# Other landing times in a kernel's build-time planner, and another table of planning parameters (attention block and gated feed-forward, one core)

## The chip, the core and the metric

The kernel runs on one core of a Trainium2 chip. The metric is the device time of one execution in microseconds. The core has TensorE (PE: matmuls, with its weight loads shown apart), VectorE (DVE), ScalarE (ACT), GpSimd (POOL) and SyncE (SP), each with a queue of its own that it works through in order. Nearly all transfers (DMAs) are issued by SP.

## The reference

For x of 2048 tokens by 512 features, in bf16:

```python
mod = (silu(c) @ w_mod)                # six rows of 512: sa, ca, ga, sb, cb, gb
h = layernorm(x) * (1 + ca) + sa
# 32 heads of 16: q, k, v = h @ wqkv; p = softmax(q k^T / 4); o = p v
x = x + ga * (o @ wo)
h = layernorm(x) * (1 + cb) + sb
x = x + gb * ((gelu(h @ w_gate) * (h @ w_up)) @ w_down)    # 512 -> 1792 -> 512
```

With 32 heads of only 16 features, the scores are 32 x 2048 x 2048 numbers that all have to be exponentiated. That is the main work.

## The kernel before

**Tiles.** The scores are cut into slots: 128 keys on the partitions by 512 columns (queries of one head, or two key tiles by 256 queries). There are 2048 slots. A round is four slots, one for each of four heads that share TensorE's array. The queries are cut into nine sets (`SETS`: seven of 256, two of 128); a unit is one set (or two merged) with one of eight head groups `qd` of four heads. For each unit the kernel goes through its rounds: scores into the PSUM tile `ps_sc`, exponential into `E`, and the product with the values into `ps_pv`; a seventeenth column of ones in the values (`vaug`) gives the softmax's sums.

**Two ways to exponentiate.** ACT takes two or three slots in one ACTIVATE (`E<-ps_sc`, 128x1024 or 128x1536; the helper's line is 377). Some rounds go to DVE instead, as one "quad": four TENSOR_SCALAR that read `ps_sc` and write uint16 bit patterns of an approximate power of two (128x512, line 389), and three more over 128x2048 that shift the bits (`shift_task`, line 1804). The four versions are weighted by scaled copies of the values (`vs`) in the product and so average out much of the approximation's error.

**Side work.** All else runs beside the scores, mostly through the PSUM tile `ps_mi`: layer norms and the projections to q, k and v of later groups, then, as sets of queries are done, the output projection, second layer norm and feed-forward of each set. The feed-forward of the first six sets streams its weights from HBM in double buffers. Exponentials of the GELU (a tanh) go to ACT as well (`wreg<-wreg`).

**The end of a unit** (`unit_end`, line 1826) normalises: the product with its sums is copied to `osb`; SP moves the sums to `den` ("db", spread over 128 partitions); DVE takes reciprocals into `rden`; SP stores them in HBM ("dc", `scr_rec<-rden`), and loads them back broadcast over 16 partitions in four pieces ("dd", `rb<-scr_rec`); DVE multiplies `osb` by `rb` into `onorm`. When the odd head groups of a set are there, SP moves them beside the even ones ("de", `onorm<-onorm`). The other names: "st" loads gate and up weights, "sd" loads scaled down weights; "se" loads the raw down weights, DVE scales them by gb, and "ws" stores them (`wd_scaled<-mreg`, seven times in a row, each after the one before, lines 995 to 1003).

**The planner.** No order is written out. When the program is built, `stream` (line 1441) places instructions one at a time on a modelled clock: it asks when each candidate could start (`probe`, line 327), takes one, and moves the clock of its engine on (`model`, line 297). The order that results is fixed in each engine's queue; at run time only semaphores hold it. For a DMA the clock has a time of issue (`ISSUE`) and a landing:

```python
self.free[eng] = t + ISSUE.get(op.stream[2:4], 450)                                   # 301
self.dma_free = max(t + 900, self.dma_free) + size / (320 if run >= 1024 else 245 if run >= 512 else 200)
op.t1 = self.dma_free + (1000 if run > 64 else 1500) + margin                          # 303
late = EARLY if qd < 6 else (0, 0, 0)                                                  # 1845, in unit_end
```

Here `margin` is the name's entry in `MARGIN` (nanoseconds; 0 if it has none), plus one of `EARLY`'s three numbers for the sums, the broadcasts and the merges of head groups below 6. A step that needs a transfer is placed on its engine's queue when the clock says that the transfer has landed (`step`, line 1312). A transfer that really lands later makes the engine stand at that step, with all that is queued behind it.

**The table.** `TUNE` has a row for each 64 slots (`rules(pos // 64)`, line 1634; rows are counted from 0, the last of the 33 stands for all beyond it). The 14 entries of a row, counted from 0:
- 0: how much work (ns) ACT must have ahead before side work or filling goes before scores
- 1: from slot 1536 on, the owed side work ("credit", in columns, at most 4096) below which a round may go to DVE
- 2: how many DVE steps may be waiting when a round is given to DVE
- 3: how long DVE may stand for a score bank before another step is put ahead
- 4 and 5: how far DVE's clock may be ahead of now (4) or of ACT's (5) when it takes scores
- 6 and 7: when the shifts of a round become urgent
- 8 and 9: how far ahead a round for DVE is picked, and how near to its unit's end it no longer is
- 10 and 11: how much credit side work needs to run, and to go ahead of scores
- 12: how fast credit accrues, in per cent
- 13: how far ahead DVE is given steps in the background

The line that gives a round to DVE (1668, cut) reads:

```python
if (len(mem) == CH or there) and c > 2 and self.free["dve"] < max(t + self.tune[4], self.free["act"] + self.tune[5]):
```

TensorE's activity is watched too: `short` (line 1427) sums the columns placed in the last 3413 ns of the clock, and where they are below `FILL` = 3700, idle stretches are filled with matmuls whose result isn't used (lines 1660 and 1755 to 1768).

Of the kernel before, what the change touches and what calls it, by code (L numbers as in the profile page):

```python
# [50 lines left out]
FLOW = sum(a + n <= 1536 for a, n in SETS)  # L51
ISSUE = {"dd": 462, "de": 630, "db": 610, "dc": 400, "st": 410, "sd": 530, "se": 530, "ws": 450, "wu": 420, "wg": 510, "wd": 480, "ou": 400, "qo": 620}
SAFE = 0
EARLY = (1500, 2500, 2000)
MARGIN = {"db": 1200, "dd": 1800, "de": 1500, "qo": 1500, "st": 1500, "sd": 1700, "se": 1700, "wd": 1700, "wu": 1500, "wg": 1500}
FIRST = (2, 1, 2, 3)
STOP = ('ln2',)
STOPAT = 0
# [2 lines left out]
STEP = 64  # L61
RULES = (600, 3500, 6, 120, 700, 150, 2, 9, 96, 30, 2, 1536, 100, 150)
TUNE = (
# [33 lines left out]
)  # L97
END = (0, None)
WAIT = 250
# [29 lines left out]
class _Recorder:  # L129
# [292 lines left out]
    def dma(self, eng, out, in_, sem, noncontig=False, late=0):  # L422
# [8 lines left out]
        run = min(int(a.ap[-1][1]) * mybir.dt.size(a.dtype) for a in (out, in_))  # L431
        return self.rec(eng, fn, [in_], [out], dma=sem, cost=(n, run, MARGIN.get(sem[:2], 0) + late))

# [36 lines left out]
class _Kernel(_Recorder):  # L470
# [967 lines left out]
    def rules(self, i):  # L1438
        self.tune = TUNE[min(i, len(TUNE) - 1)]

# [385 lines left out]
    def unit_end(self, u, acc):  # L1826
# [17 lines left out]
        sem = b + 4 * (o > 0)  # L1844
        late = EARLY if qd < 6 else (0, 0, 0)
        s2 = self.scr2[b, P * o:P * o + 4 * L]
# [261 lines left out]
```

## Time and profile before

| | us |
|---|---|
| runs shown (3) | 808.4, 812.86, 815.13 |
| median | 812.86 |
| the profiled execution | 810.3 |
| its span, first to last instruction | 808.6 |
| ACT busy | 776.8 |
| DVE busy | 752.3 |
| PE busy | 750.5 |
| mean granted TensorE clock | 0.996 |

Times in the profile are microseconds from the span's start. A group is written line, engine, operation, output<-inputs (buffer numbers left out), how many times. "Idle before" is the time in which the engine stood just ahead of such an instruction, with what released it. The helpers that record instructions each have one line (364 matmul, 377 activation, 389 tensor_scalar, 427 DMA), so groups are told apart by their tiles. Consecutive instructions of one engine overlap a little: their mean durations add up to more than the busy time.

### The profile page before, as it was taken

How to read it: one execution, taken by the hardware profiler on the slowest of the kernel's cores; microseconds unless marked ns; L12 is line 12 of the kernel's file. 1: busy time of each engine (PE TensorE's matmuls, PEld its weight loads, DVE VectorE, ACT ScalarE, POOL GpSimd, SP SyncE). 2: the span in 40 equal slices, each digit the busy share in tenths (PEclk: the TensorE clock that was granted, in tenths of full speed). 3: DMA queues.
4: the chain of work that ended last, by engine and by line, in shares of the span. 5: the costliest groups of instructions: out<-in, count | busy, mean ns of one | idle time of the engine just before them, and what ended most of it. 6: DMA issues, size and time to landing. Idle time of an engine off the chain costs nothing.

```text
span 808.6 us, 37540 instructions
## 1 busy us (share of the span) xinstructions
PE 750.5 (93%) x17260; PEld 374.8 (46%) x17264; DVE 752.3 (93%) x1521; ACT 776.8 (96%) x734; POOL 4.6 (1%) x13
## 2 busy tenths in 40 slices
PE   8899999998989998999999999988999999989998
PEld 4333334433544454444543554344434554446666
DVE  7877899999999999999999999999998999999973
ACT  6999999999999999999999999999999999999972
POOL 2000000000000000000000000000000000000000
PEclk9999999999999999999999999999999999999999
DMA  9100112221541144104420442043223622200000
GB/s 295 66 15 8 25 50 74 75 58 32 148 145 29 39 128 134 34 16 133 129 65 16 140 121 54 22 128 114 62 64 104 189 83 76 71 10 13 18 12 15
DMA packets 97904, 60.92 MB, mean 75 GB/s; under 512 B 16913, under 2 KB 95378, under 8 KB 97746
## 3 DMA queue, kind: packets, MB, share of 16 engines
q1 hardware_dynamic: 97216, 57.99, 25.2%
q8 instruction: 135, 2.21, 1.1%
q10 hardware_dynamic: 530, 0.53, 0.2%
q14 instruction: 23, 0.19, 0.1%
HBM read 51.74 MB, written 4.18 MB: 69 GB/s over the span
## 4 chain that ended last, share of the span: by engine, by line
ACT 81%; PE 13%; DVE 3%; DMA 2%; issue 1%; SPq 0%; DVEq 0%
ACT E L377 78%; PE ps_sc L364 5%; PE ps_mi L364 4%; PE ps_pv L364 3%; ACT wreg L377 3%; DMA scr_rec<-rden 1%; DMA xs<-in_A_x_dram 0%; DVE mreg L389 0%; DMA mreg<-in_B_w_up_dram 0%; SPq L427 0%; DMA rb<-scr_rec 0%; DVE st L417 0%; DVE wreg L398 0%; DVE hreg L389 0%; PE ps_mi L368 0%
## 5 line engine op out<-in xcount | busy, mean ns | idle before, releaser
L377 ACT ACTIVATE E<-ps_sc 128x1024 bf16<-128x1024 f32 (+2 forms) x688 | 750.8, 1295 | 17.8 <-PE ps_sc L364 17.2
L364 PE MATMUL ps_sc<-qo,kT 32*128 32x256 bf16 (+2 forms) x2048 | 202.0, 273 | 19.8 <-ACT E L377 17.6
L364 PE MATMUL ps_sc<-qT,kT 32*128 32x256 bf16 (+3 forms) x2048 | 202.0, 274 | 17.7 <-ACT E L377 14.3
L364 PE MATMUL ps_pv<-E,vaug 128*17 128x256 bf16 (+2 forms) x3168 | 151.5, 274 | 2.7 <-DVE vaug L398 1.1
L389 DVE TENSOR_SCALAR dreg<-ps_sc 128x512 uint16<-128x512 f32 x204 | 138.2, 687 | 4.6 <-PE ps_sc L364 4.0
L364 PE MATMUL ps_mi<-wreg,mreg 128*32 128x256 bf16 x2816 | 110.0, 275 | 5.2 <-DVE wreg L398 1.7
L364 PEld LDWEIGHTS ps_sc<-qT,kT 32*128 32x128 bf16 (+1 forms) x2048 | 62.7, 92 | 109.8 <-ACT E L377 89.4
L364 PEld LDWEIGHTS ps_sc<-qo,kT 32*128 32x128 bf16 x2048 | 63.1, 92 | 106.5 <-ACT E L377 87.7
L364 PEld LDWEIGHTS ps_pv<-E,vaug 128*17 128x17 bf16 x3168 | 61.0, 89 | 58.9 <-issue 40.8
L389 DVE TENSOR_SCALAR kq<-ps_sc 128x512 uint16<-128x512 f32 x112 | 76.3, 688 | 8.0 <-PE ps_sc L364 7.4
L364 PEld LDWEIGHTS ps_mi<-wreg,mreg 128*32 128x32 bf16 x2816 | 64.1, 96 | 38.6 <-issue 21.5
L364 PE MATMUL ps_pv<-mreg,vs 128*17 128x256 bf16 (+2 forms) x1544 | 69.6, 267 | 0.5 <-issue 0.5
L389 DVE TENSOR_SCALAR mreg<-ps_sc 128x512 uint16<-128x512 f32 x100 | 67.7, 687 | 1.7 <-PE ps_sc L364 1.2
L389 DVE TENSOR_SCALAR mreg<-dreg 128x2048 uint16<-128x2048 uint16 x91 | 61.5, 686 | 0.0
L364 PEld LDWEIGHTS ps_pv<-mreg,vs 128*17 128x17 bf16 x1544 | 35.2, 91 | 9.6 <-issue 3.4
L364 PE MATMUL ps_mi<-hreg,wreg 128*32 128x512 bf16 (+1 forms) x496 | 37.3, 382 | 0.4 <-DVE vaug L398 0.2
L381 DVE TENSOR_TENSOR wreg<-wreg 128x1024 bf16<-128x1024 bf16 (+1 forms) x56 | 34.6, 618 | 0.0
L394 DVE SCALAR_TENSOR_TENSOR wreg<-wreg,ps_mi 128x512 bf16<-128x512 bf16 x49 | 33.5, 683 | 0.6 <-PE ps_mi L364 0.2
L398 DVE CAST wreg<-ps_mi 128x512 bf16<-128x512 f32 x49 | 33.6, 686 | 0.5 <-PE ps_mi L364 0.2
L389 DVE TENSOR_SCALAR mreg<-mreg 128x2048 uint16<-128x2048 uint16 x46 | 31.1, 684 | 0.0
L389 DVE TENSOR_SCALAR mreg<-kq 128x2048 uint16<-128x2048 uint16 x45 | 30.7, 686 | 0.1
L377 ACT ACTIVATE wreg<-wreg 128x1024 bf16<-128x1024 bf16 (+1 forms) x28 | 29.8, 1065 | 0.0
(202 smaller groups left out, 786.9 us busy)
## 6 DMA issues: line engine op xcount, KB each, us to landing
mreg<-in_B_w_up_dram SPq DMA_DIRECT2D x46, 256.0 KB, 3.1
mreg<-in_B_w_gate_dram SPq DMA_DIRECT2D x42, 256.0 KB, 3.7
dreg<-wd_scaled SPq DMA_DIRECT2D x18, 256.0 KB, 3.4
rb<-scr_rec SPq DMA_DIRECT2D x116, 32.0 KB, 2.0
mreg<-wd_scaled SPq DMA_DIRECT2D x12, 256.0 KB, 4.2
ereg<-wd_scaled SPq DMA_DIRECT2D x12, 256.0 KB, 4.1
mreg<-in_w_mod_dram SPq DMA_DIRECT2D x1, 2048.0 KB, 12.2
out_dram<-xs SPq DMA_DIRECT2D x15, 128.0 KB, 2.0
```

What stands on the lines that cost most here:

```text
L364: return self.rec("pe", lambda e: e.matmul(out, lhsT, rhs, start=start, stop=stop, tile_position=tp), [lhsT, rhs], [out], cost=(n, int(rhs ...
L377: return self.rec("act", lambda e: e.activation(out, in_, func, scale=scale, **kw), rd, wr, cost=self.cost("act", out, [in_], "act"))
L381: return self.rec(eng, lambda e: e.tensor_tensor(out, a, b, op), [a, b], [out], cost=self.cost(eng, out, [a, b], "tt"))
L389: return self.rec(eng, lambda e: e.tensor_scalar(out, a, s1, s2, **kw), rd, [out], cost=self.cost(eng, out, [a], "ts") + 60 * (len(rd) - 1 ...
L394: return self.rec("dve", lambda e: e.scalar_tensor_tensor(out, a, s, b, op0=op0, op1=op1), rd, [out], cost=self.cost("dve", out, [a, b], " ...
L398: return self.rec(eng, lambda e: e.tensor_copy(out, in_), [in_], [out], cost=self.cost(eng, out, [in_], "ts"))
```

## The change

Only three constants change; no function does. `EARLY` and `MARGIN` hold the landing times that the planner's clock assumes, and `TUNE` is another table, found by a search that charged stretches with few TensorE columns. Since the planner places every instruction by them, the order in all queues after the first microseconds may differ, and so may the number of rounds that go to DVE. What is computed is the same, but for which rounds are exponentiated on which engine.

```diff
-EARLY = (1500, 2500, 2000)
-MARGIN = {"db": 1200, "dd": 1800, "de": 1500, "qo": 1500, "st": 1500, "sd": 1700, "se": 1700, "wd": 1700, "wu": 1500, "wg": 1500}
+EARLY = (800, 1000, 800)
+MARGIN = {"db": 1200, "dd": 1800, "de": 1500, "qo": 1500, "st": 2300, "dc": 1500, "ws": 1500, "sd": 2000, "se": 1700, "wd": 1700, "wu": 1500, "wg": 1500}
```

All rows of the table but a few change. These are rows 0 to 6, 15 to 19 and 29 to 32, the old ones first:

```diff
 TUNE = (
-    (600, 3500, 6, 120, 700, 150, 2, 9, 96, 30, 2, 1536, 100, 150),
-    (600, 3500, 6, 120, 700, 150, 2, 9, 96, 30, 2, 1536, 100, 150),
-    (600, 3000, 4, 120, 700, 300, 2, 9, 96, 30, 2, 1536, 80, 150),
-    (600, 3000, 5, 60, 700, 150, 2, 9, 96, 30, 2, 1536, 80, 150),
-    (600, 3000, 5, 60, 700, 150, 3, 9, 96, 30, 2, 1536, 125, 150),
-    (600, 3000, 5, 60, 1100, 150, 3, 9, 96, 30, 2, 1536, 80, 150),
-    (600, 3500, 6, 120, 900, 450, 2, 16, 64, 30, 2, 1536, 110, 150),
...
-    (600, 4097, 6, 200, 900, 150, 2, 9, 128, 38, 2, 1536, 125, 400),
-    (600, 4097, 6, 200, 900, 300, 2, 6, 128, 38, 2, 1536, 125, 150),
-    (600, 4097, 6, 0, 900, 300, 2, 6, 128, 34, 0, 1536, 125, 0),
-    (450, 4097, 6, 0, 900, 300, 2, 6, 48, 34, 0, 1536, 125, 0),
-    (450, 4097, 6, 0, 900, 300, 2, 6, 48, 34, 0, 1536, 125, 0),
...
-    (600, 3500, 6, 120, 700, 150, 2, 9, 96, 30, 2, 1536, 100, 150),
-    (1000, 3500, 6, 120, 500, 150, 2, 6, 96, 24, 2, 1536, 100, 150),
-    (450, 4097, 6, 300, 1100, -100, 1, 9, 96, 30, 4, 1536, 100, 150),
-    (450, 4097, 6, 300, 1100, -100, 1, 9, 96, 30, 4, 1536, 100, 150),
+    (1000, 4097, 6, 120, 700, 150, 2, 9, 96, 30, 2, 1536, 100, 150),
+    (600, 3500, 6, 120, 700, 150, 2, 3, 96, 38, 2, 1536, 100, 150),
+    (600, 3500, 6, 120, 1100, -100, 2, 6, 96, 27, 2, 1536, 100, 400),
+    (1000, 3500, 6, 120, 1100, 450, 3, 9, 96, 27, 2, 1536, 125, 400),
+    (1000, 3500, 6, 120, 1100, 450, 3, 9, 96, 27, 2, 1536, 125, 400),
+    (1000, 3500, 8, 120, 1100, 300, 3, 9, 96, 27, 2, 2500, 125, 400),
+    (1000, 3500, 8, 120, 1100, 300, 3, 9, 96, 27, 2, 2500, 125, 400),
...
+    (600, 3500, 6, 120, 700, 150, 0, 9, 96, 30, 2, 800, 100, 150),
+    (450, 3500, 6, 120, 700, 150, 0, 9, 96, 30, 2, 800, 100, 150),
+    (450, 2500, 6, 0, 700, 150, 0, 9, 128, 30, 1, 800, 125, 250),
+    (450, 2500, 7, 60, 700, 150, 0, 9, 128, 30, 1, 800, 125, 150),
+    (300, 2500, 10, 60, 700, 0, 0, 9, 128, 24, 1, 2500, 125, 150),
...
+    (600, 2500, 6, 0, 700, 450, 1, 9, 64, 27, 1, 1536, 125, 150),
+    (600, 2500, 3, 200, 1100, 450, 1, 3, 64, 27, 2, 1536, 125, 150),
+    (600, 3500, 6, 120, 700, 450, 2, 9, 96, 27, 0, 1536, 100, 150),
+    (600, 3500, 6, 120, 700, 450, 2, 9, 96, 27, 0, 1536, 100, 150),
 )
```

31 rows, old and new, of the table TUNE are left out of this document.

## The prediction, made before the changed kernel ran

> **What bounds the kernel now.** I read the page's head, then the busy time by stretch, then the waits by engine, then the chain of work. First the page:
>
> ```profile
> span 808.6 us, 37540 instructions
> PE 750.5 (93%) x17260; PEld 374.8 (46%) x17264; DVE 752.3 (93%) x1521; ACT 776.8 (96%) x734; POOL 4.6 (1%) x13
> ACT 81%; PE 13%; DVE 3%; DMA 2%; issue 1%; SPq 0%; DVEq 0%
> ```
>
> ScalarE (ACT) is busy for 96% and carries 81% of the chain. The stretches show where its other 4% lies. Columns: stretch, length, then busy time of PE, weight loads, DVE, ACT and POOL, the granted clock, DMA share and GB/s.
>
> ```profile
> 15.40:100.00 84.60, 77.58 (x1376) 29.43 (x1376) 70.06 (x184) 84.17 (x78) 0.31 (x1) 0.98 0.14 46
> 100.00:200.00 100.00, 93.65 (x2149) 40.44 (x2145) 97.41 (x190) 100.00 (x93) 0.00 (x0) 1.00 0.22 61
> 200.00:300.00 100.00, 93.15 (x2242) 47.89 (x2246) 96.72 (x183) 98.80 (x94) 0.00 (x0) 1.00 0.34 97
> 300.00:400.00 100.00, 93.04 (x2213) 46.49 (x2201) 96.98 (x182) 99.81 (x94) 0.00 (x0) 1.00 0.32 91
> 400.00:500.00 100.00, 93.93 (x2180) 46.34 (x2180) 98.15 (x184) 100.00 (x96) 0.00 (x0) 1.00 0.29 79
> 500.00:600.00 100.00, 93.15 (x2160) 44.99 (x2156) 98.93 (x187) 100.00 (x96) 0.00 (x0) 1.00 0.28 76
> 600.00:700.00 100.00, 94.16 (x2130) 46.99 (x2126) 96.50 (x186) 98.68 (x92) 0.00 (x0) 0.98 0.35 101
> 700.00:781.30 81.30, 75.53 (x2386) 46.23 (x2379) 75.24 (x160) 80.63 (x74) 0.00 (x0) 1.00 0.10 26
> 781.30:808.60 27.30, 23.18 (x357) 19.71 (x348) 11.91 (x34) 7.05 (x13) 0.00 (x0) 1.00 0.04 12
> ```
>
> Between 15.4 us (first exponential) and 781.3 us (last one) ACT idles for 0.43 + 1.20 + 0.19 + 1.32 + 0.67 = 3.8 us of 766. So the middle is bound by the number of score columns that ACT exponentiates; mending waits can bring 3.8 us there at most. Only moving columns to DVE brings more. DVE idles for 14.5 us before 100 us, for 15.3 us between 100 and 700, and for 6.1 us up to 781.3.
>
> What a moved column costs is in the groups by shape (count | busy, mean ns of one | idle before) and in DVE's order of time (start us, length us):
>
> ```profile
> L377 ACT ACTIVATE E<-ps_sc 128x1024 bf16<-128x1024 f32 x412 | 413.8, 1137 | 2.3 <-PE ps_sc L364 2.2
> L377 ACT ACTIVATE E<-ps_sc 128x1536 bf16<-128x1536 f32 x268 | 394.8, 1560 | 2.8 <-PE ps_sc L364 2.3
> 227.54 0.69 DVE L381 TENSOR_TENSOR wreg<-wreg 128x1024 bf16<-128x1024 bf16 x1
> 228.14 0.69 DVE L389 TENSOR_SCALAR kq<-ps_sc 128x512 uint16<-128x512 f32 x1
> 228.74 0.68 DVE L394 SCALAR_TENSOR_TENSOR wreg<-wreg,ps_mi 128x512 bf16<-128x512 bf16 x1
> 230.57 0.69 DVE L381 TENSOR_TENSOR onorm<-osb,rb 128x512 bf16<-128x512 f32 x1 [1.15 <-DMA rb<-scr_rec]
> ```
>
> One slot of 512 columns is 1560 - 1137 = 423 ns of ACT. A round is four slots: 1.7 us of ACT. On DVE it takes four score readings and three shifts, which follow each other every 0.60 us (227.54, 228.14, 228.74): 4.2 us.
>
> **The change, part by part.**
>
> *Stores of reciprocals ("dc", +1.5 us).* Line 303 has assumed that they land 0.90 + 0.04 + 1.50 = 2.44 us after issue; now 3.94. The trace has one that came late. The fence shows the chain of work there, ACT in order of time, two rows of the DMA issues (the last figure is the median from issue to landing) and SP's waits:
>
> ```profile
> 221.47 4.71 DMA scr_rec<-rden
> 228.38 2.07 DMA rb<-scr_rec
> 230.57 0.69 DVE onorm L381
> 234.94 1.45 ACT L377 ACTIVATE E<-ps_sc 128x1536 bf16<-128x1536 f32 x1 [1.14 <-PE ps_sc L364]
> scr_rec<-rden SPq DMA_DIRECT2D x29, 8.0 KB, 1.6
> rb<-scr_rec SPq DMA_DIRECT2D x116, 32.0 KB, 2.0
> SPq L427 <- DMA scr_rec<-rden: 34.8, 24, 3.1
> ```
>
> The store took 4.71 us, SP stood behind it, the multiplication in DVE's queue waited 1.15 us, and ACT then lacked 1.14 us. With 1.5 us more, the multiplication stands later in DVE's order and other steps fill its place; the weight loads queued behind SP's wait go ahead of it. Gain 1.1 us, bounds 0 (another late store elsewhere, median 1.6) and 1.2. [...]
>
> *EARLY cut (sums -0.7, broadcasts -1.5, merges -1.2 us for head groups below 6).* Sums 5.14 to 4.44 us, broadcasts 6.30 to 4.80, merges 5.50 to 4.30. With the store's +1.5 the way from reciprocal to multiplication stays the same for these groups; for groups 6 and 7 it is 1.5 us longer. Broadcasts land after 2.0 us (median); no landing of sums is shown. Bounds for the sums: a gain of 0, as no one waits for them, and, if they landed as late as the worst store (4.71 against 4.44), 0.3 us of DVE at each of 32 sums, 9.6 us of DVE or two rounds, 3.4 us of ACT. I take 0: the nearest row, a small load into SBUF, has 2.0. Longer ways in groups 6 and 7 delay the projection of a query set by 1.5 us; its cover is the feed-forward work of the set before. If that cover is gone, the nearest row prices it at ACT's 1.14 us for each of six sets, 6.8 us; I take 0, and keep the 6.8 for the range.
>
> *Weight loads ("st" +0.8, "sd" +0.3, "ws" +1.5 us).*
>
> ```profile
> PE ps_mi L364 <- DMA mreg<-in_B_w_up_dram: 1.6, 1, 1.6
> mreg<-in_B_w_up_dram SPq DMA_DIRECT2D x46, 256.0 KB, 3.1
> L427 SPq DMA_DIRECT2D wd_scaled<-mreg x7: 359/376/433, 110.5 to 159.3; - x7
> L427 SPq DMA_DIRECT2D mreg<-in_B_w_gate_dram x42: 367/380/1653, 178.3 to 643.5; - x42
> ```
>
> "st" goes from 4.47 to 5.27 us assumed; the median is 3.1. One wait of 1.6 us on PE falls into 300 to 340 us, where ACT lost 0.19: gain 0.2 (0 to 0.2). The weights are double buffered and 42 loads spread over 465 us, 11 us each, so 0.8 us stays hidden. The stores of the scaled weights stand seven in a row: 7 x 1.5 = 10.5 us, covered by the 19 us between the last of them (159.3) and the first load that follows (178.3); without that cover it would be PE's side work that starts late, not ACT. I take 0.
>
> *Few columns.* In two places TensorE fell to half its clock (stretches of 1 us, columns as above):
>
> ```profile
> 89.00:90.00 1.00, 1.00 (x15) 0.14 (x7) 1.00 (x3) 1.00 (x2) 0.00 (x0) 0.50 0.00 0
> 93.00:94.00 1.00, 1.00 (x19) 0.27 (x15) 0.48 (x2) 0.57 (x2) 0.00 (x0) 1.00 0.08 16
> 621.00:622.00 1.00, 0.62 (x7) 0.43 (x10) 0.92 (x3) 1.00 (x2) 0.00 (x0) 0.68 0.09 8
> 623.00:624.00 1.00, 1.00 (x22) 0.17 (x15) 0.35 (x1) 0.59 (x1) 0.00 (x0) 0.50 0.47 82
> 625.00:626.00 1.00, 1.00 (x33) 0.56 (x31) 0.53 (x1) 0.67 (x2) 0.00 (x0) 1.00 0.63 205
> ```
>
> ACT lost 0.43 us behind the first and 0.41 + 0.33 behind the second: 1.2 us. A table that avoids thin stretches can save these; one drawn otherwise can bring two others: bounds -1.2 and +1.2. I take -0.6. [...]
>
> *The table itself.* It sets when a round goes to DVE and when side work goes ahead of scores; how many rounds come out isn't to be read from it. Bounds: all idle DVE time (14.5 + 15.3 + 6.1 = 35.9 us, 8 rounds of 4.2) would take 8 x 1.7 = 13.6 us off; as many lost would add them. The best hundred (500 to 600) leaves DVE 1.07 us idle. The six hundreds at that level would free 15.3 - 6.4 = 8.9 us, two rounds. In front, part of DVE's idle time is waits for projections on PE:
>
> ```profile
> DVE kT L398 <- PE ps_mi L364: 3.3, 6, 1.2
> DVE vaug L398 <- PE ps_mi L364: 2.6, 4, 1.9
> ```
>
> Rows 2 to 6 of the new table hasten this side work (row 3: work accrues at 125 instead of 80, DVE may run 1100 ns ahead instead of 700). Of these I take one round, -1.7 us: nearest to the hundreds, which are all but full. The last 27.3 us (feed-forward of the last rows) hold the same work: 0.
>
> **Sum:** -1.1 - 0.2 - 0.6 - 1.7 = -3.6 us. The profiled execution took 810.3 us (span 808.6 and 1.7 around it): 806.7. The median of the runs shown lies 2.6 above that execution (812.86); the same for the changed kernel gives 809.3 us.
>
> **The rivals.**
> 1. Faster by over 1%: the table fills the front. 14.5 us idle before 100 us hold three rounds, the hundreds two more: 5 x 1.7 = 8.5 us, with 1.9 from the waits, 812.9 - 10.4 = 802.5. For it: DVE's 70.06 busy of 84.60 there. Against: this idle time hangs on data, and every later stretch is full to 96%.
> 2. Slower by over 1%: rounds are refused near the end. From slot 1536 on a round is taken only while the owed side work is below the table's second entry; rows 29 and 30 lower it from 3500 to 2500, row 31 from 4097 (which the debt, capped at 4096, never reached) to 3500. Those three rows hold 3 x 64 = 192 slots, 48 rounds; ACT has 412 x 2 + 268 x 3 = 1628 of the 2048 slots by the groups above, so DVE has a fifth, about ten of these rounds. Each refused one hands 1.7 us back to ACT. With 1.9 saved at the waits, (8.1 + 1.9) / 1.7 = six refused rounds of the ten decide; at eight it is 812.9 - 1.9 + 13.6 = 824.6. For it: ACT has no slack (98.68 of 100 in 600 to 700). Against: a DVE that scores less works the side work off and the bar lifts.
> 3. The assumptions don't matter: one broadcast and one weight load were waited for among hundreds, so orders differ and time doesn't: 813, within 1%.
>
> **How the numbers follow.** 1% (8 us) is about what a measurement of this kernel can tell from no change; the runs shown span 808.4 to 815.13. Forecast 0.36 and rival 3 0.12: within 1% 0.48, with 804.7 to 820 as their range. Rival 1 0.29, rival 2 0.23. A range of 799 to 823 goes from rival 1 with two more rounds (802.5 - 3.4) to rival 2 at seven rounds (822.9), takes in the 6.8 us of the unknown delays, and leaves some 0.15 out.
>
> **What would show it.** Right: no wait of the multiplications for broadcasts, no PE wait of over 1 us for weights, no stretch at 0.50, and fewer than 1628 slots on ACT, by four for the round. Wrong: DVE waiting for sums or broadcasts several times; more slots on ACT; a longer stretch behind the last exponential than 27.3 us; ACT idle by over 4 us in the middle.

## The result, and the profile after

The changed kernel took 807.99 us (median of 12 runs, 806.82 to 809.53), the kernel before 811.59 (12 runs, 808.40 to 815.13). The ratio is 0.9956, with a 95% interval of 0.9941 to 0.9971: 3.6 us less, within 1%. The forecast was 809.3 us and within 1%. The runs also lie closer together: 2.7 us apart instead of 6.7.

The page of the changed kernel, to be held against the one of before (its execution took 808.1 us):

```profile
span 806.4 us, 37404 instructions
PE 749.7 (93%) x17203; PEld 373.9 (46%) x17203; DVE 748.8 (93%) x1514; ACT 778.1 (96%) x729; POOL 4.9 (1%) x13
ACT 79%; PE 13%; DVE 6%; DMA 1%; issue 1%; SPq 0%; DVEq 0%
```

ACT is as much the bound as it was. The same stretches of the changed kernel:

```profile
15.40:100.00 84.60, 77.51 (x1385) 29.25 (x1371) 72.07 (x186) 84.60 (x80) 0.56 (x1) 1.00 0.15 47
100.00:200.00 100.00, 94.59 (x2173) 41.38 (x2173) 96.99 (x192) 100.00 (x92) 0.00 (x0) 1.00 0.21 58
200.00:300.00 100.00, 92.70 (x2204) 46.31 (x2196) 97.49 (x183) 99.92 (x93) 0.00 (x0) 1.00 0.34 97
300.00:400.00 100.00, 93.35 (x2184) 47.19 (x2182) 96.02 (x180) 99.39 (x93) 0.00 (x0) 0.98 0.31 86
400.00:500.00 100.00, 94.07 (x2214) 47.00 (x2218) 96.94 (x184) 99.53 (x92) 0.00 (x0) 1.00 0.31 84
500.00:600.00 100.00, 93.94 (x2154) 44.61 (x2142) 98.16 (x184) 99.93 (x96) 0.00 (x0) 1.00 0.28 76
600.00:700.00 100.00, 92.98 (x2100) 45.66 (x2100) 95.81 (x186) 99.70 (x94) 0.00 (x0) 1.00 0.38 111
700.00:781.30 81.30, 76.52 (x2402) 47.90 (x2398) 73.36 (x160) 80.24 (x72) 0.00 (x0) 1.00 0.07 13
781.30:806.40 25.10, 21.56 (x301) 18.21 (x293) 11.18 (x30) 6.76 (x13) 0.00 (x0) 1.00 0.04 13
```

The clock column has one place below 1.00 (0.98 in 300 to 400) where before had two. The groups by shape count ACT's slots:

```profile
L377 ACT ACTIVATE E<-ps_sc 128x1536 bf16<-128x1536 f32 x282 | 416.2, 1562 | 2.7 <-PE ps_sc L364 2.4
L377 ACT ACTIVATE E<-ps_sc 128x1024 bf16<-128x1024 f32 x393 | 398.0, 1143 | 1.1 <-PE ps_sc L364 0.9
```

282 x 3 + 393 x 2 = 1632 slots, against 1628: DVE got one round *fewer*, not one more. So the 2.2 us between the two profiled spans must come from elsewhere. ACT's order of time shows where. Below are the start of the exponentials and the table load that follows the last of them, the kernel before ahead of the changed one:

```profile
15.38 1.02 ACT L377 ACTIVATE E<-ps_sc 128x1024 bf16<-128x1024 f32 x1 [0.67 <-PE ps_sc L364]
781.25 1.28 ACT L377 ACT_TABLE_LOAD   x1
```

```profile
14.96 2.37 ACT L377 ACTIVATE E<-ps_sc 128x1024 bf16<-128x1024 f32 x2 [0.67 <-PE ps_sc L364]
780.93 1.28 ACT L377 ACT_TABLE_LOAD   x1
```

- The start is 0.42 us earlier. That is chance: in seven profiles of this document it lies between 14.90 and 15.54 us, and the kernel below that keeps the order of before with one multiplication near 230 us moved, starts at 14.90.
- In the middle ACT idles 2.6 us instead of 3.8: -1.2.
- In the middle ACT works 780.93 - 14.96 - 2.6 = 763.4 us instead of 781.25 - 15.38 - 3.8 = 762.1: +1.3. The lost round is priced at 1.7 by the prediction.
- From the last exponential to the end it is 806.4 - 780.93 = 25.5 us instead of 808.6 - 781.25 = 27.35: -1.9.

Together -0.4 - 1.2 + 1.3 - 1.9 = -2.2. The end, which the prediction took at nothing, is the largest term. The waits for landings in the changed kernel:

```profile
DVE onorm L381 <- DMA rb<-scr_rec: 0.4, 1, 0.4
DVE rden L401 <- DMA den<-osb: 0.3, 1, 0.3
PE ps_mi L364 <- DMA mreg<-in_B_w_up_dram: 0.7, 1, 0.7
PEld ps_mi L364 <- DMA mreg<-in_B_w_up_dram: 1.0, 1, 1.0
```

None of them is above 1.0 us; before had 1.15 and 1.58.

### The profile page after: what moved, and what is told of

It reads as the page before. It is cut to its first block, busy times and chain, and to the rows that moved or that the text cites. A ratio compares the mean times of both kernels' runs of the same rounds, so it can differ in the third digit from the quotient of the medians.

```text
span 806.4 us, 37404 instructions
## 1 busy us (share of the span) xinstructions
PE 749.7 (93%) x17203; PEld 373.9 (46%) x17203; DVE 748.8 (93%) x1514; ACT 778.1 (96%) x729; POOL 4.9 (1%) x13
## 4 chain that ended last, share of the span: by engine, by line
ACT 79%; PE 13%; DVE 6%; DMA 1%; issue 1%; SPq 0%; DVEq 0%
ACT E L377 76%; PE ps_sc L364 5%; PE ps_mi L364 5%; PE ps_pv L364 3%; ACT wreg L377 2%; DVE mreg L389 1%; DVE dreg L389 1%; DVE wreg L394 1%; DVE wreg L398 1%; DMA xs<-in_A_x_dram 0%; DMA mreg<-in_B_w_up_dram 0%; DVE wreg L381 0%; DVE kq L389 0%; DVE hreg L381 0%; DVE hreg L389 0%
## 5 line engine op out<-in xcount | busy, mean ns | idle before, releaser
L364 PE MATMUL ps_sc<-qo,kT 32*128 32x256 bf16 (+2 forms) x2048 | 195.8, 273 | 18.3 <-ACT E L377 14.9
L364 PE MATMUL ps_sc<-qT,kT 32*128 32x256 bf16 (+3 forms) x2048 | 196.3, 273 | 16.7 <-ACT E L377 13.2
L364 PE MATMUL ps_pv<-E,vaug 128*17 128x256 bf16 (+2 forms) x3188 | 154.4, 273 | 1.3 <-DVE vaug L398 0.5
L389 DVE TENSOR_SCALAR dreg<-ps_sc 128x512 uint16<-128x512 f32 x200 | 135.4, 683 | 5.4 <-PE ps_sc L364 4.3
L364 PEld LDWEIGHTS ps_sc<-qo,kT 32*128 32x128 bf16 x2048 | 60.6, 92 | 108.7 <-ACT E L377 90.6
L364 PEld LDWEIGHTS ps_sc<-qT,kT 32*128 32x128 bf16 (+1 forms) x2048 | 60.9, 92 | 103.7 <-ACT E L377 79.6
L364 PE MATMUL ps_pv<-mreg,vs 128*17 128x256 bf16 (+2 forms) x1504 | 67.0, 270 | 1.3 <-DVE mreg L389 1.2
L364 PEld LDWEIGHTS ps_pv<-mreg,vs 128*17 128x17 bf16 x1504 | 33.0, 91 | 14.5 <-issue 5.7
L389 DVE TENSOR_SCALAR mreg<-mreg 128x2048 uint16<-128x2048 uint16 x49 | 33.0, 680 | 0.0
L389 DVE TENSOR_SCALAR mreg<-kq 128x2048 uint16<-128x2048 uint16 x40 | 27.0, 682 | 0.3 <-PE ps_pv L364 0.2
```

What stands on the lines that cost most here:

```text
L364: return self.rec("pe", lambda e: e.matmul(out, lhsT, rhs, start=start, stop=stop, tile_position=tp), [lhsT, rhs], [out], cost=(n, int(rhs ...
L389: return self.rec(eng, lambda e: e.tensor_scalar(out, a, s1, s2, **kw), rd, [out], cost=self.cost(eng, out, [a], "ts") + 60 * (len(rd) - 1 ...
```

## The experiments

Twelve kernels ran. All times are medians beside the kernel before on the same chip, which took 810.4 to 810.9 us in these comparisons.

**The two halves of the change.** First, only `EARLY` and `MARGIN` are new (here and below, the changed lines are shortened or put in short form):

```diff
-EARLY = (1500, 2500, 2000)
+EARLY = (800, 1000, 800)
...
+MARGIN = {... "st": 2300, "dc": 1500, "ws": 1500, "sd": 2000 ...}
 TUNE = (   # as before
```

> The new landing times with the table of before. Its program has 1644 slots on ACT (before 1628). Theory of the sum (the prediction's: landing times and table act one beside the other): the waits at 230 and 320 us go, -1.3 us, so 810.3 beside 811.6. Theory of the fit (a table is good only for the very landing times it was searched with): four rounds of 1.7 us come back to ACT, +6.8 us, and new waits on top: 816 to 822.

It took 825.5 us, ratio 1.0185 (1.0163 to 1.0206): 15 us slower. Then only `TUNE` is new:

```diff
 MARGIN = {...}   # as before
-TUNE = (   # the old rows
+TUNE = (   # the new rows
```

> The new table with the landing times of before. Its program has 1636 slots on ACT. Theory of the sum: the table's terms alone, -2.3 us (810 to 809). Theory of the fit: two rounds back to ACT, +3.4 us, and new waits: 814 to 820.

It took 816.4 us, ratio 1.0079 (1.0062 to 1.0095). The halves cost 15 and 6 us; together they gain 3.6. The theory of the sum is out. The theory of the fit named the second time rightly; the first half was worse than its 816 to 822. The groups by shape of the margins-only kernel:

```profile
L377 ACT ACTIVATE E<-ps_sc 128x1536 bf16<-128x1536 f32 x297 | 435.7, 1551 | 7.7 <-PE ps_sc L364 7.1
L377 ACT ACTIVATE E<-ps_sc 128x1024 bf16<-128x1024 f32 x376 | 381.4, 1124 | 3.2 <-PE ps_sc L364 2.9
L377 ACT ACTIVATE E<-ps_sc 128x512 bf16<-128x512 f32 x7 | 4.3, 610 | 9.6 <-PE ps_sc L364 9.5
```

Six of the seven single ones belong to the feed-forward's end, so ACT has 297 x 3 + 376 x 2 + 1 = 1644 slots: four rounds of 1.7 us came back to it, 6.8 us. Its idle time ahead of the two large groups is 7.7 + 3.2 us, where before had 2.8 + 2.3: 5.8 us more. Both together are 12.6 of the 15 us.

**How little it takes.** One assumption is changed by 0.1 us, and nothing else:

```diff
-MARGIN = {"db": 1200, ...
+MARGIN = {"dc": 100, "db": 1200, ...
```

> Before, with a single assumption changed by next to nothing: stores of reciprocals land 0.1 us later in the planner's clock. Its program has 1636 slots on ACT (before 1628). Theory of the sum: nothing, 810.4. Theory of the fit: any difference draws a new order, for which the table wasn't chosen: two rounds back to ACT, +3.4 us, and new waits: 813 to 818.

It took 821.3 us, ratio 1.0132 (1.0105 to 1.0159), more than the theory of the fit allowed. In the groups by shape:

```profile
L377 ACT ACTIVATE E<-ps_sc 128x1536 bf16<-128x1536 f32 x282 | 416.2, 1555 | 6.3 <-PE ps_sc L364 6.1
L377 ACT ACTIVATE E<-ps_sc 128x1024 bf16<-128x1024 f32 x395 | 399.3, 1127 | 4.8 <-PE ps_sc L364 4.2
```

These are 1636 slots, two rounds more, and 11.1 us idle ahead of the two groups instead of 5.1. A change that moves no transfer on the chip by itself costs 10.6 us, three times the gain of the whole change under study. So each of the three pairings of a table with landing times other than its own was slower, by 0.8% to 1.9%.

**The wait of the multiplication.** The order of before is kept, and one instruction is moved: the multiplication that waited at 230.57 us stands three places later on DVE.

```diff
+calls.insert(three_dve_steps_later, calls.pop(index_of_the_eighth_onorm_product))
```

> The order of before with one instruction moved: the multiplication that waited for the broadcast at 230.57 us stands three places later in DVE's order. Theory of the sum: its wait of 1.15 us goes, and with it ACT's 1.14 us at 234.94: 810.5 beside 811.6. Rival: that loss is covered, since the late store comes elsewhere in other runs: no change, 811.6.

810.4 us, ratio 0.9997 (0.9984 to 1.0009): no gain that can be told from nothing, though the interval reaches 1.3 us less and so doesn't rule the forecast out. Its profile has no wait for broadcasts left, but others in their place (ACT in order of time, then a wait of TensorE):

```profile
225.39 4.39 ACT L379 ACTIVATE E<-ps_sc 128x1024 bf16<-128x1024 f32 x4 [1.48 <-PE ps_sc L366]
234.77 1.45 ACT L379 ACTIVATE E<-ps_sc 128x1536 bf16<-128x1536 f32 x1 [0.46 <-PE ps_sc L366]
PE ps_mi L366 <- DMA mreg<-in_B_w_up_dram: 3.0, 2, 2.0
```

In this execution weight loads came late: TensorE waited 1.96 us for one until 224.18 us, and ACT 1.48 us behind it. The late store of reciprocals, by contrast, wasn't a thing of one execution. Eight profiles have the order of before up to added matmuls or this one moved product: before, this run and the six runs that fill places in it, told below. In all eight the store near 221 us took 3.0 to 5.0 us, where the median store of before took 1.6. What differs is how long the multiplication then waits and what ACT loses near 234 us. In the four profiles without such a wait (this one among them) ACT still stood 0.33 to 0.54 us there; with waits of 0.37, 0.60, 1.00 and 1.15 us it stood 0.81, 0.76, 1.13 and 1.14 us. So only a part of the 1.14 us hung on the wait.

**The thin places.** Again the order of before, with 52 matmuls added that add zeros to the open sum in `ps_pv` and so keep TensorE's columns up: between 86 and 89 us, and between 618 and 621.

```diff
+for i, call in enumerate(calls):                  # the order of before
+    ...
+    for _ in range(groups_after.get(i, 0)):       # four matmuls a group
+        matmul(pv[32 * j:32 * j + 17, 0:W], zero[:, 0:17], xs[:, 15, 0:W], start=False, stop=False)
```

> The order of before with 52 matmuls added that add zeros to the open sum in ps_pv: five groups of four between 86 and 89 us, eight between 618 and 621 us, 1.9 us of TensorE in all at 0.21 and 0.11 us a group. Theory that the half clock costs: the granted clock stays at 1.00 in both places, and ACT gets back 0.4 to 1.2 us: 810.4 to 811.2, and the runs lie closer together than 808.4 to 815.1. Rival: the added matmuls delay scores as much as the clock did: 811.6 or up to 1 us more.

807.3 us, ratio 0.9966 (0.9954 to 0.9978): 2.8 us less (1.8 to 3.7), nearly the gain of the whole change, from filling two places. The mean granted clock of its seven runs is 0.9996, against 0.9964 for the kernel before beside it. Three stretches of 1 us behind the filled places, in its profile, now have the clock at 1.00:

```profile
89.00:90.00 1.00, 1.00 (x19) 0.33 (x16) 1.00 (x3) 0.83 (x1) 0.00 (x0) 1.00 0.00 0
621.00:622.00 1.00, 1.00 (x38) 0.56 (x30) 0.61 (x2) 0.87 (x2) 0.00 (x0) 1.00 0.09 33
623.00:624.00 1.00, 1.00 (x34) 0.39 (x22) 1.00 (x2) 1.00 (x2) 0.00 (x0) 1.00 0.58 119
```

The control puts the same 52 matmuls where TensorE has work enough.

> The control to the run before: the same 52 matmuls that add zeros, put into the order of before where TensorE has work enough (five groups of four near 66 to 69 us, eight near 500 to 502 us). Theory of the half clock (what helped was the clock staying up at the thin places): no gain, 810.4 to 811.5. Rival (the added matmuls help by shifting the order against landings, wherever they are): about -3 us again, 807.

810.5 us, ratio 1.0001 (0.9979 to 1.0024), runs from 807.4 to 816.2. So matmuls of this kind alone gain nothing; where they stand matters. Its profile also shows what a late weight load can start (stretches of 1 us):

```profile
321.00:322.00 1.00, 0.00 (x0) 0.00 (x0) 1.00 (x2) 0.94 (x1) 0.00 (x0) 1.00 0.18 37
322.00:323.00 1.00, 0.32 (x8) 0.15 (x8) 0.79 (x2) 0.00 (x0) 0.00 (x0) 1.00 0.27 59
324.00:325.00 1.00, 1.00 (x18) 0.25 (x10) 0.36 (x1) 0.91 (x1) 0.00 (x0) 0.50 0.75 219
326.00:327.00 1.00, 1.00 (x18) 0.29 (x18) 0.85 (x3) 0.95 (x2) 0.00 (x0) 0.50 0.82 241
```

TensorE stood (0.00, 0.32) for a load, ACT lost a whole microsecond, and then the clock fell to 0.50. Each place alone:

> Before with the zero matmuls at the first thin place alone (five groups of four, 512 columns, between 86 and 89 us). Filled together with the second, it gave -3.2 us. If each fall costs about the same: -1.6 us, 809.1 beside 810.7. If a fall early in the run is made good later by ACT's lead: nothing, and all of it at the second place.

> Before with the zero matmuls at the second thin place alone (eight groups of four, 256 columns, between 618 and 621 us). If each fall costs about the same: -1.6 us, 809.1 beside 810.7; if the early one is made good later, -3 us, 807.7.

The first gave 0.9992 (0.9972 to 1.0012), the second 0.9982 (0.9963 to 1.0001). Neither can be told from nothing by itself; their sum, 0.26%, fits the 0.34% of both, but which place weighs more stays open. The profiles agree on the clock: of the eight in the order of before, the four with the first place filled have no fall there, and three of the four others have one; the same holds for the second place.

What a fall costs is seen in the runs of the kernel before themselves. Over the 93 runs of it in the four comparisons, the granted clock of a run and its time go together (correlation -0.83):

| mean clock of the run | runs | median us |
|---|---|---|
| 1.000 | 15 | 808.9 |
| 0.998 | 20 | 809.7 |
| 0.996 | 40 | 810.9 |
| 0.995 | 4 | 811.8 |
| 0.994 | 6 | 812.5 |
| 0.993 | 3 | 812.8 |
| 0.992 | 4 | 814.8 |
| 0.991 | 1 | 814.5 |

One fall of 3.4 us at half clock (as from 88.9 to 92.3 us in the profile of before) lowers the mean by 0.5 x 3.4 / 809 = 0.0021. A line through the runs gives 1.3 us for each 0.002. That includes what goes with a fall, such as the late load just ahead of it in the control (3.0 us). By this line the clock makes an estimated 2.1 of the 2.8 us that filling both places gained. And the run with one assumption changed by 0.1 us had a mean clock of 0.989: an estimated 4.9 of its 10.6 us go with more falls. That overlaps with its longer idle time and isn't a term beside it.

**The changed kernel, filled.** The same treatment at its five thinnest places (92 matmuls of 256 columns):

> The changed kernel's order with 92 such matmuls of 256 columns at its own five thinnest places (88, 195, 299, 355 and 705 us; 2.5 us of TensorE in all). Theory of the half clock: the changed kernel has about one fall left (0.50 at 356 to 359 us), so it gains less than the order of before did: -0.5 to -1.5 us, 806.5 to 805.5 on a chip where the changed kernel takes 807. Rival (the falls don't matter by now): 807 to 808.

807.7 us, ratio 0.9963 (0.9947 to 0.9978), the clock at 1.000 in 11 of 12 runs. The changed kernel without it stands at 0.9956 (0.9941 to 0.9971). Nothing is gained, as the rival had it, though the changed kernel's mean clock was 0.9981. That the added 2.5 us of TensorE work eats up what the clock gives is an argument, not shown. Its profile also has four stops of TensorE of the kind told next, 0.4 to 1.0 us each between 759 and 780 us, where the changed kernel's has one, of 0.7. No kernel here is shown to be faster than the changed one.

**The end, and a stop without a cause in the profile.**

> Before with both places filled, and eight more groups just ahead of the matmul that waits for a weight load near 320 us (1.6 us in the profile of before, 3.0 us in that of the control, where the clock fell behind it and ACT lost 2.4 us). Theory of the half clock: a load that comes late costs most through the fall behind it, so -3.2 and some -0.5 to -1.5 more, 807 to 806 beside 810.7. Rival (the wait itself is the cost): no more than with two places, 807.5.

812.0 us, ratio 1.0014 (0.9993 to 1.0035): the third place gains nothing, and what the first two gave is gone. The clock was high (mean 0.9987), so it isn't the falls in the middle. TensorE's order of time near the end of this kernel:

```profile
781.52 0.34 PE L367 MATMUL ps_pv<-mreg,vs 128*17 128x128 bf16 x11
783.18 0.28 PE L367 MATMUL ps_pv<-mreg,vs 128*17 128x128 bf16 x5 [1.32 <-issue]
```

TensorE stops between the 11th and the 12th of sixteen products and waits for nothing that the profile shows ("issue"). The last product of the scores hangs on it, and with it the whole end: 29.0 us. The kernel before has two such stops there, after the 3rd and the 15th product of a row of sixteen:

```profile
778.57 0.39 PE L364 MATMUL ps_pv<-mreg,vs 128*17 128x128 bf16 x13 [0.46 <-issue]
782.04 0.22 PE L364 MATMUL ps_pv<-ereg,vs 128*17 128x128 bf16 x1 [0.44 <-issue]
```

To see whether the place is set by the number of instructions ahead of it, the last kernel has as many as the one just shown, but with the eight groups at 500 us instead of 320.

> The two thin places filled as in the run that gave -3.2 us, and the eight groups that the last run put near 320 us moved to where TensorE has work enough, near 500 to 502 us. The number of TensorE instructions ahead of the end is that of the last run, in whose profile TensorE stood 1.32 us in the end, between the 11th and the 12th of 16 products, waiting for nothing that the profile shows, with 29.0 us from the last exponential to the end (26.3 with 64 instructions fewer). [...] Rival (the eight groups near 320 us hurt where they stood): an end of 26.3 us, 807.5 to 808.

813.4 us, ratio 1.0026 (1.0004 to 1.0049), and TensorE's order of time:

```profile
785.03 0.34 PE L367 MATMUL ps_pv<-mreg,vs 128*17 128x128 bf16 x11
786.71 0.28 PE L367 MATMUL ps_pv<-mreg,vs 128*17 128x128 bf16 x5 [1.33 <-issue]
```

The same stop, at the same product, as long as before: with the count kept and the work ahead rearranged, the place stayed. The end is 812.6 - 784.78 = 27.8 us here, not the 26.3 of the rival; the other 1.2 us of the run just before this one (29.0) came with a fall of the clock inside its end, from 785.3 to 788.7 us (its mean over that end is 0.94, here 1.00). The run with the first two places filled has 104 instructions more than before (52 weight loads, 52 matmuls) and no such stop between 772 and 786 us, and its end is 26.3 us instead of 27.35; the changed kernel has none either, with 25.5. So up to about 1.1 us of what filling gained may be the end and not the clock. That is one profile against one, and the control speaks against a full 1.1: it has the same shift and the same end (26.3 us), a mean clock of 0.9972, and gained nothing in the median (1.7 us less to 1.9 more). Nor do the ends account for all that the last two runs lost against the run with two places filled.

What makes TensorE stop at these places isn't shown: the profile names no releaser. Nor does an equal count settle how long such a stop is. The run with the moved multiplication has the TensorE instructions of the kernel before and stops at the same two products, but for other lengths:

```profile
781.67 0.39 PE L366 MATMUL ps_pv<-mreg,vs 128*17 128x128 bf16 x13 [0.18 <-issue]
785.41 0.22 PE L366 MATMUL ps_pv<-ereg,vs 128*17 128x128 bf16 x1 [0.71 <-issue]
```

Over the whole span TensorE stands 2.4 us in five such stops in that run, and 1.6 us in four in the kernel before.

**The new table's last rows alone.**

```diff
-TUNE[28:33] of before
+TUNE[28:33] of the changed kernel
```

> Before, with the new table's last five rows (28 to 32) alone. Its program has 1632 slots on ACT, one round more than before. Rival 2 of the prediction (rows 29 to 31 refuse rounds): only one of about ten is refused, +1.7 us: 812. Theory of the end (the new rows shorten what follows the last exponential, 25.5 against 27.3 us in the two profiles): -1.8 + 1.7, so 810.4. Theory of the fit: +1.7 and new waits: 812 to 816.

810.8 us, ratio 1.0010 (0.9985 to 1.0034). ACT has 1632 slots, and 25.5 us follow the last exponential. One round lost and the shorter end balance, as the theory of the end had it, as far as an interval from 1.2 us less to 2.8 more can tell; rival 2's mass of refused rounds isn't there.

## Why the prediction was right, and where its steps failed

The time held: 809.3 forecast, 808.0 measured, within 1% of the kernel before as said. That the sum of -3.6 us is also the measured difference is luck. Of its four terms one had the wrong sign, one wasn't borne out, two were priced wrongly or not measured apart, and the largest piece was put at 0; they made up for each other. Adding a term for the landing times to one for the table was itself wrong: each half alone made the kernel slower, by 15 and 6 us. Of its signs of being right, the short waits for weights came and broadcasts were waited for once (0.4 us); but one stretch at 0.50 was left, and ACT had more slots and not fewer, which it had named as a sign of being wrong.

- *Stores of reciprocals, -1.1 us.* Not borne out. The step said that the wait of one multiplication, once gone, gives ACT's 1.14 us back. With the wait taken away in an unchanged order the time changed by -0.03% (-0.16% to 0.09%). The place was read rightly, for the store there was late in all eight profiles of this order (and took 4.4 us in the changed kernel's); but ACT stands 0.33 to 0.54 us there without the wait too.
- *EARLY, 0.* Right as far as shown: one wait of 0.3 us for sums, one of 0.4 us for broadcasts.
- *Weight loads, -0.2 us.* Mis-sized. One execution had shown 1.6 us of PE's wait. The same order showed 0.2 to 3.8 us in seven further profiles, and behind 3.0 us the clock fell. The changed kernel's waits are short (0.7 and 1.0), but the share of the longer assumption in that wasn't measured apart.
- *Few columns, -0.6 us.* The mechanism was right, the size was off. The step priced a fall by ACT's idle time just behind it (1.2 us for two). Over 93 runs a fall goes with 1.3 us, and filling both places gave 2.8 us (1.8 to 3.7), of which up to 1.1 may belong to the end. With the mean clock at 0.9966 before and 0.9981 after, the changed kernel's share is 0.0015 x 1.3 / 0.002 = 1.0 us by the line through the runs. The runs of the kernel before differ (15 of 93 had no loss, 4 had a mean clock of 0.992), but the loss was there in most. In its profile the two falls last from 88.9 to 92.3 us and from 621.4 to 624.8, in the changed kernel's the one fall from 355.9 to 359.3: 3.4 us each.
- *The table, -1.7 us by one round.* Wrong in sign: one round less on DVE, +1.3 us in ACT's middle. Idle DVE time in front did fall, from 14.5 to 12.5 us, without a round for it.
- *The end, 0.* Wrong: -1.9 us. TensorE's stops of 0.46 and 0.44 us stood in the trace before the prediction; they lie in the end's chain, and the changed kernel's profile doesn't have them there. By the other profiles about 1.0 us goes with the stops (the order of before has an end of 26.3 to 26.6 us in the four without a stop between 772 and 786 us), and about 0.8 with the new last rows (25.5 us in the run with them alone, also without a stop).
- *The 2.6 us between profile and median.* They were carried over as they stood. With twelve runs it was 1.3 for the kernel before and -0.1 for the changed one. That the changed kernel's fewer falls bring its median nearer to its better executions is likely, but not shown apart.

Rival 3, that the assumptions don't matter, had a time within 1% too, but its mechanism was the most mistaken: 0.1 us in one of them moved the time by 1.3%. Rivals 1 and 2 didn't come.

Open is how the 3.6 us divide: about 1.0 for fewer falls (a line, not an experiment on the changed kernel), 1.9 less 1.3 for the end and the lost round in one pair of profiles, and the rest in waits that differ from run to run.

## What to carry to other kernels

Where a planner builds the order of a whole program, its parameters and its assumptions are one thing: test them together, and take any change of either, however small, for a new draw. Price a stall by runs with and without it, not by the idle time beside it in one trace, and see in several profiles whether it comes back; look at each run's clock first. And compare what lies behind the last piece of the bounding engine's work, for the longest steps of such a comparison may stand there.

## What the runs showed that was not expected

- TensorE stops for 0.2 to 1.3 us without a cause that the profile names. Two kernels with the same number of TensorE instructions, but 32 of the matmuls moved by 180 us, stopped between the same two products (1.32 and 1.33 us); the kernel with 64 instructions fewer ahead had no such stop between 772 and 786 us. So matmuls added far ahead went with such a stop in the chain that sets the end (29.0 and 27.8 us), or with none (26.3).
- In the kernel before the clock fell to 0.50 behind a stretch in which TensorE was never idle for more than 0.47 us at a time, only thinly used. Its busy share between 86 and 89 us was 0.65 to 0.96, with 32 matmuls of a single column between 86.2 and 87.6 us, and the clock fell right behind:

```profile
86.00:87.00 1.00, 0.96 (x22) 0.56 (x19) 0.96 (x2) 1.00 (x2) 0.00 (x0) 1.00 0.00 0
87.00:88.00 1.00, 0.65 (x19) 0.47 (x16) 1.00 (x3) 1.00 (x2) 0.00 (x0) 1.00 0.00 0
88.00:89.00 1.00, 0.88 (x15) 0.48 (x19) 0.96 (x4) 1.00 (x2) 0.00 (x0) 0.94 0.00 0
89.00:90.00 1.00, 1.00 (x15) 0.14 (x7) 1.00 (x3) 1.00 (x2) 0.00 (x0) 0.50 0.00 0
```
